# State tokens' products with the data's high and low words side by side, and a reordered end of the layer-one stage, in an attention and two-layer MoE kernel

## The chip, the cores and the metric

The kernel runs on one core of one Trainium2 chip. The metric is device time in microseconds of one execution, the median of several runs. Engines are named as in the profile: PE is TensorE's matmul, PEld its weight load, DVE is VectorE, ACT is ScalarE, POOL is GpSimd, SP is SyncE, which here issues most DMAs (SPq is its queue).

## What is computed

Inputs are `x` (8, 8, 512, 64) and `state` (8, 8, 32, 64): 8 batch entries, 8 heads, 512 ordinary tokens and 32 state tokens each. The reference, cut to its core:

```python
# attention, per batch entry and head
xread = softmax(x @ state.T / 8) @ state       # 512 tokens
sread = softmax(state @ x.T / 8) @ x           # 32 state tokens
x = concat(xread, sread)                       # to (4352, 512): 8 * 544 tokens
# first layer
h = np.maximum(x @ w_in, 0.0)                  # w_in  512 x 2048
x = h * h @ w_out                              # w_out 2048 x 512
# second layer
a = x @ w1                                     # 512 x 1024
b = x @ w2                                     # 512 x 1024
out = ((a * b) @ w3) @ w_out2                  # 1024 x 1024, 1024 x 512
```

Everything is float32 (weights reach the kernel as float64). The kernel keeps float32 precision by splitting a number into a high word and a low word (both float32r, a type of which TensorE takes one column in one pass) and adding three products: high times high, low times high, high times low.

## The kernel before, in words

**Tokens.** The 8 x 512 ordinary tokens are the batches c = 0 to 7, with tiles 512 columns wide. The 8 x 32 = 256 state tokens of all batch entries form a ninth batch, c = B = 8, with tiles 256 columns wide (NT9). The change touches the products of c = B alone.

**Splits and passes.** `split` (L80) makes a ScalarE copy that rounds to the high word (L81) and a VectorE subtraction that gives the low word (L82). `PASSES` (L84) lists the three pairs of words. Split tiles are 128 x 2 x 512, high words in the first half, low words in the second.

**Layer one.** `h_tile(c, f)` (L477) makes one of 16 tiles of hidden units. For c = B (L493 to L502) it splits the 512 x 128 piece of w_in, then does 4 products over k, three matmuls of 256 columns each, into half a PSUM bank of the pair "h". `act_h` (L469) then does Relu out of PSUM, Square, and a split into `ghl`. `y_tile(c, f)` (L513) multiplies with w_out's row f into four banks y0 to y3, three matmuls for each d, and at the last f copies each bank to a tile `yo` (two buffers), from which it is stored to DRAM (`y_scr`). The loop over `order` (L717) keeps y two tiles behind h with the list `pend`; after the loop two y tiles are left in it.

**The product w34 = w3 @ w_out2.** `w3_split(kk)` (L749) splits one of eight rows of the transposed w3 into two tiles, which share two buffers each (tags sw0 and sw1) with the w_in pieces. `w34_rows(kk)` (L763) does 24 matmuls of 512 columns into a bank of the pair "h", splits the result, and after each second row makes sums and differences that go to DRAM (`w34u`). The eight rows are taken in the loop at L1206; while one is multiplied, the next is split. Before that loop, the two y tiles left are done (L1203). Halfway, `make_w` (L829) splits the first half of w1 and w2 with their sums.

**Layer two.** It runs in two passes s = 0, 1, each over half of the 1024 inner units. Ordinary batches are taken in pairs with a Strassen-like scheme: `load_pair` and `make_pair` (L854, L863; 14 splits and 8 differences) make the right sides, `quad` (L941) multiplies into banks qa, qd, qe and qc, `out_pair` (L1071) multiplies with w34. The state tokens go ahead of the pairs: `load9` (L984) reads their y from DRAM, `make9` (L992) splits it into `z` tiles, `ab9(m)` (L1000, m = 0 to 3) makes a and b as two times four products in two banks of y0 to y3 (two m at a time hold banks), and multiplies them: a ScalarE copy of the first bank, a VectorE product with the second, and a split. `out9` (L1030) multiplies the four results with w34. In pass 0, `load9` puts its data into tag s0 of pool `bp`, which is opened (L1216) over the memory that w34's pool leaves.

**What sets the order.** The instructions of each engine run in one fixed order, made when the kernel is built: a scheduler takes them by their place in the text, and lets a later one go ahead where an earlier one isn't ready by its own estimate. `tc.issue_after(ins)` keeps a block's instructions on the engine of `ins` behind `ins`. At run time each engine is strictly in order, and so is SP's queue of DMAs, each of which waits at the head until its buffers are ready.

Of the kernel before, what the change touches and what calls it, by code (L numbers as in the profile page):

```python
# [20 lines left out]
def kernel(  # L21
# [17 lines left out]
    nc = tc.nc  # L39
# [428 lines left out]

    def act_h(c, f, ph, n):  # L469
        r = pa.tile([P, 512], F32, tag="r", bufs=2, name="r")  # L470
        nc.scalar.activation(r[:, :n], ph[:, :n], ACTF.Relu)
        t = pa.tile([P, 2, 512], F32R, tag="ghl", bufs=3, name="ghl")
        nc.scalar.activation(r[:, :n], r[:, :n], ACTF.Square)  # L473
        done.append(split(t[:, HI, :n], t[:, LO, :n], r[:, :n]))
        g_t[c, f] = t

    def h_tile(c, f):  # L477
        ph = bank_h(f"ph{c}_{f}_")
        if c < B:
            fg, m = f // 4, f % 4  # L480
            k = 0
            for g in range(G):
                s, a = SW[c, fg, g], aT_t[c, g]
                for wi, ai in PASSES:
                    mm = nc.tensor.matmul(
                        ph, s[:, wi, m * P:(m + 1) * P], a[:, ai, :],
                        start=(k == 0), stop=(k == 3 * G - 1),
                    )
                    k += 1
            h_mms.append(mm)  # L490
            act_h(c, f, ph, 512)
        else:
            cols = slice((f % 4) * P, (f % 4 + 1) * P)  # L493
            t = pa.tile([P, 2, ND, P], F32R, tag=f"sw{f % 2}", bufs=2, name="w9")
            split(t[:, HI], t[:, LO], win_t[f // 4][:, :, cols])
            for k in range(ND):
                for i, (wi, xi) in enumerate(PASSES):
                    nc.tensor.matmul(
                        ph[:, :NT9], t[:, wi, k, :], x9_t[k // 2][:, xi, k % 2, :],
                        start=(k == 0 and i == 0), stop=(k == ND - 1 and i == 2),  # L500
                    )
            act_h(c, f, ph, NT9)  # L502

    x9_t = []

# [7 lines left out]
    def y_tile(c, f):  # L513
        n = 512 if c < B else NT9
        part, (f0, f1) = [(i, sg) for i, sg in enumerate(segs[c]) if sg[0] <= f < sg[1]][0]
        if f == f0:
            for d in range(ND):
                y_ps[c, d] = bank_y(d, f"y{d}")
        if wo_t[f] is None:
            close_splits()  # L520
        t = g_t.pop((c, f))
        for d in range(ND):
            for k, (wi, gi) in enumerate(PASSES):
                nc.tensor.matmul(  # L524
                    y_ps[c, d][:, :n], wo_t[f][:, wi, d * P:(d + 1) * P], t[:, gi, :n],
                    start=(f == f0 and k == 0), stop=(f == f1 - 1 and k == 2),
                )
            if f == f1 - 1:
                pool, tag = (pa, "yo") if d < 2 or c >= B - 1 else (att, "yo2")
                o = pool.tile([P, 512], F32, tag=tag, bufs=2, name="yo")  # L530
                if d % 2 and c > 1:
                    nc.vector.tensor_copy(o[:, :n], y_ps[c, d][:, :n])
                else:
                    nc.scalar.copy(o[:, :n], y_ps[c, d][:, :n])
                nc.sync.dma_start(y_scr[c][part][:, d, :], o[:, :n])
# [213 lines left out]
    def w3_split(kk):  # L749
        src = stage["w3", kk].rearrange("p h (d k q) -> p k (h d) q", d=2, q=NS)  # L750
        for half in range(2):
            t = pa.tile([P, 2, 4, 4, NS], F32R, tag=f"sw{half}", bufs=2, name="w3T")
            split(t[:, HI], t[:, LO], src[:, 4 * half:4 * half + 4])
            w3T[kk, half] = t.rearrange("p s k d q -> p s (k d q)")

    NH = DM // 2
    NB = N1 // 4
# [242 lines left out]
    def ab9(m):  # L1000
        pss = [bank_y(2 * i + m % 2, "ab") for i in range(2)]
        for i in range(2):
            for d in range(ND):
                w = W[f"A{i + 1}{d // 2 + 1}", d % 2]
                for k, (wi, vi) in enumerate(PASSES):
                    nc.tensor.matmul(  # L1006
                        pss[i][:, :NT9], w[:, wi, m * P:(m + 1) * P], Y[B, d][:, vi, :NT9],
                        start=(d == 0 and k == 0), stop=(d == ND - 1 and k == 2),
                    )
        a = bp.tile([P, 512], F32, tag="s0", bufs=2, name="a")  # L1010
        nc.scalar.copy(a[:, :NT9], pss[0][:, :NT9])
        nc.vector.tensor_tensor(out=a[:, :NT9], in0=pss[1][:, :NT9], in1=a[:, :NT9], op=ALU.mult)
        if m % 2 == 0:
            left["c9"] = z_tile(5 if m == 0 else 1, "c9").rearrange("p h (d n) -> p d h n", d=2)
        t = c_t[B, m] = left["c9"][:, m % 2]
        split(t[:, HI], t[:, LO], a[:, :NT9])

    o_scr = {}
    o_in = {}
# [180 lines left out]

    rows = list(range(N1 // 2, N1)) + list(range(N1 // 2))
    w3_split(rows[0])
    while pend:  # L1203
        y_tile(*pend.pop(0))
    raw = load_w(0)
    for i, kk in enumerate(rows):  # L1206
        if i + 1 < N1:
            w3_split(rows[i + 1])
        if i + 4 < N1:
            load_w3(rows[i + 4])  # L1210
        w34_rows(kk)
        if i == 3:
            for job in make_w(raw):
                job()
# [1 line left out]
    bp = ctx.enter_context(tc.tile_pool(name="bp", bufs=1, reuse_waits="tile"))  # L1216

    turns = [(3, 4), (5, 6), (7, 2), (0, 1)]
    raw9 = load9(bp, "s0")
    raw = load_pair(*turns[0])  # L1220
    make9(raw9)
    while rest:
        rest.pop()()
    for job in make_pair(raw):
        job()
    for s, todo in enumerate((turns, turns[::-1])):
        if s == 1:
            for t in range(NT9 // P):
# [56 lines left out]
```

## Time and profile before

| what | value |
|---|---|
| median of 3 runs | 1220.3 us (1218.64 to 1220.49) |
| the profiled execution's own time | 1219.03 us |
| its span, first to last instruction | 1217.3 us |
| granted TensorE clock, mean | 0.999 of full speed |
| DMA | 150.66 MB moved, 124 GB/s mean |
| stage of the state tokens' layer one | about 612 to 667 us |
| stage of w34 | about 667 to 712 us |
| ab9 and out9, pass 0 | 715 to 733 us |
| ab9 and out9, pass 1 | 963 to 981 us |

The profile is of one execution; times in it count from its first instruction. A row of the timeline gives the start, how long the merged instructions take, the engine, the line, the operation and its tiles; a wait ahead of the row stands in brackets, with the instruction that ended it. "Mean ns" of a matmul includes its way through the pipeline, so that matmuls which follow each other closely overlap in it.

### The profile page before, as it was taken

What the parts mean: (1) busy time and instruction counts of PE and PEld (TensorE: products, weight loads), DVE (VectorE), ACT (ScalarE), POOL (GpSimd) and SP (SyncE); (2) the same over time, 40 slices, a digit from 0 to 9 for tenths busy, and PEclk for the clock granted to TensorE, in tenths of its full rate; (3) what the DMA queues carried; (4) which work ended last, traced back from release to release, by engine and by line L of the source; (5) the groups of instructions that cost most, each with busy time, mean ns of one, the idle gap of its engine ahead of it and who ended that gap; (6) DMA issues with size and microseconds to landing.
All of it is one profiled execution on the core that took longest, in us unless ns stands there. A gap on an engine that the chain in (4) does not pass through costs nothing.

```text
span 1217.3 us, 18891 instructions
## 1 busy us (share of the span) xinstructions
PE 1201.4 (99%) x7174; PEld 999.6 (82%) x7174; DVE 869.4 (71%) x1594; ACT 662.2 (54%) x1220; POOL 109.4 (9%) x163
## 2 busy tenths in 40 slices
PE   7999999999999999999999999999999999999998
PEld 5677777777778777778899888989898989898988
DVE  6968877677586766742435875878696957877877
ACT  6877466555464655654656653546363635453542
POOL 0000001322421121100000000000000000211110
PEclk9999999999999999999999999999999999999999
DMA  9445664835446397630413642223232540716244
GB/s 260 138 140 173 159 184 145 185 113 130 129 127 156 106 184 155 154 53 35 121 53 113 222 156 98 81 93 104 70 104 70 191 138 20 155 30 144 49 74 138
DMA packets 147922, 150.66 MB, mean 124 GB/s; under 512 B 81016, under 2 KB 107128, under 8 KB 147320
## 3 DMA queue, kind: packets, MB, share of 16 engines
q1 hardware_dynamic: 120968, 106.20, 29.6%
q0 software_dynamic: 26576, 43.00, 15.6%
q8 instruction: 56, 0.92, 0.3%
q14 instruction: 34, 0.28, 0.1%
q10 hardware_dynamic: 288, 0.26, 0.1%
HBM read 99.61 MB, written 55.05 MB: 127 GB/s over the span
## 4 chain that ended last, share of the span: by engine, by line
PE 89%; DMA 4%; DVE 3%; ACT 3%; SPq 1%; issue 0%; DVEq 0%; ACTq 0%
PE y L524 29%; PE qa L945 11%; PE qd L945 7%; PE oa L1096 5%; PE od L1096 4%; PE qc L945 4%; PE qe L945 4%; PE ps_sw L454 2%; PE ab L1006 2%; PE oe L1096 2%; PE oc L1096 2%; DMA yraw<-yscr 1%; DMA raw<-in_moe_w_in_dram 1%; PE po L1036 1%; PE ps_r L400 1%; PE ps_s L320 1%
## 5 line engine op out<-in xcount | busy, mean ns | idle before, releaser
L524 PE MATMUL y<-ghl,wo 128*128 128x512 f32 (+1 forms) x1728 | 398.9, 380 | 0.5 <-ACT ghl L81 0.5
L524 PEld LDWEIGHTS y<-ghl,wo 128*128 128x128 f32 x1728 | 310.3, 188 | 74.9 <-issue 13.4
L82 DVE TENSOR_TENSOR ghl<-r,ghl 128x512 fp32r<-128x512 f32 (+1 forms) x144 | 95.1, 660 | 163.2 <-ACT ghl L81 138.7
L953 ACT COPY s<-qa 128x512 f32<-128x512 f32 x96 | 56.5, 589 | 180.1 <-PE qa L945 179.3
L945 PE MATMUL qa<-yq,wq 128*128 128x512 f32 x576 | 143.7, 389 | 0.0
L945 PEld LDWEIGHTS qa<-yq,wq 128*128 128x128 f32 x576 | 107.7, 188 | 22.0
L945 PE MATMUL qd<-yq,wq 128*128 128x512 f32 x384 | 97.4, 389 | 0.0
L82 DVE TENSOR_TENSOR z<-q,z 128x512 fp32r<-128x512 f32 x112 | 74.3, 687 | 23.7 <-ACT z L81 23.6
L473 ACT ACTIVATE r<-r 128x512 f32<-128x512 f32 (+1 forms) x144 | 87.7, 609 | 3.2
L81 ACT CAST ghl<-r 128x512 fp32r<-128x512 f32 (+1 forms) x144 | 86.0, 597 | 3.6
L945 PEld LDWEIGHTS qd<-yq,wq 128*128 128x128 f32 x384 | 72.1, 188 | 15.0
L1136 POOL DMA_DIRECT2D out_dram<-o x24 | 28.6, 1597 | 598.2 <-DVE o L1126 598.0
L81 ACT CAST z<-q 128x512 fp32r<-128x512 f32 x112 | 68.1, 625 | 20.2 <-PE oe L1096 7.4
L957 DVE TENSOR_TENSOR s<-qa,s 128x512 f32<-128x512 f32 x32 | 22.1, 692 | 69.8 <-ACT s L953 69.8
L82 DVE TENSOR_TENSOR yq<-yraw,yq 128x512 fp32r<-128x512 f32 x98 | 64.6, 686 | 4.2 <-ACT yq L81 4.2
L81 ACT CAST yq<-yraw 128x512 fp32r<-128x512 f32 x98 | 59.3, 625 | 12.5 <-DVE yraw L874 7.6
L945 PE MATMUL qe<-yq,wq 128*128 128x512 f32 x192 | 48.7, 389 | 0.0
L945 PE MATMUL qc<-yq,wq 128*128 128x512 f32 x192 | 48.7, 389 | 0.0
L770 PE MATMUL ps_w<-wo,w3T 128*128 128x512 f32 x192 | 44.0, 390 | 0.3 <-ACT u L81 0.3
L899 DVE TENSOR_TENSOR q<-q,q 128x512 f32<-128x512 f32 x64 | 43.1, 684 | 0.0
L770 PEld LDWEIGHTS ps_w<-wo,w3T 128*128 128x128 f32 x192 | 35.9, 188 | 8.1 <-ACT u L81 0.7
L945 PEld LDWEIGHTS qc<-yq,wq 128*128 128x128 f32 x192 | 36.0, 188 | 7.5
(598 smaller groups left out, 2059.5 us busy)
## 6 DMA issues: line engine op xcount, KB each, us to landing
yraw<-yscr SPq DMA_DIRECT2D x56, 256.0 KB, 5.4
yscr<-yo SPq DMA_DIRECT2D x52, 256.0 KB, 3.1
raw<-in_moe_w_out_dram SPq DMA_DIRECT2D x16, 512.0 KB, 4.3
raw<-in_moe_w_dram POOLq DMA_DIRECT2D x64, 128.0 KB, 3.5
raw<-in_moe_w_dram POOLq DMA_DIRECT2D x16, 512.0 KB, 5.0
raw<-in_moe_w_in_dram SPq DMA_DIRECT2D x12, 512.0 KB, 4.2
out_dram<-o SPq DMA_DIRECT2D x24, 256.0 KB, 2.7
out_dram<-o POOLq DMA_DIRECT2D x24, 256.0 KB, 6.6
```

The costliest lines, as they stand in the source:

```text
L81: nc.scalar.copy(hi, src)
L82: return nc.vector.tensor_tensor(out=lo, in0=src, in1=f32(hi), op=ALU.subtract)
L454: mm = nc.tensor.matmul(pss[r][k * NS:(k + 1) * NS, cols], stT[rows, b, k, :], win_t[fg][rows, k, cols], start=True, stop=True, tile_posit ...
L473: nc.scalar.activation(r[:, :n], r[:, :n], ACTF.Square)
L524: nc.tensor.matmul(y_ps[c, d][:, :n], wo_t[f][:, wi, d * P:(d + 1) * P], t[:, gi, :n], start=(f == f0 and k == 0), stop=(f == f1 - 1 and k ...
L770: nc.tensor.matmul(ps, t[:, wi, (j % 4) * P:(j % 4 + 1) * P], wo2_t[j][:, vi, :], start=(j == 0 and k == 0), stop=(j == N1 - 1 and k == 2),)
L899: return nc.vector.tensor_tensor(out=t, in0=a, in1=b, op=ALU.subtract)
L945: nc.tensor.matmul(ps, W[w, kt][:, wi, m * P:(m + 1) * P], Y[v, kt][:, vi, :], start=(first and kt == 0 and k == 0), stop=(last and kt == ...
L953: left["copy"] = nc.scalar.copy(t, ps)
L1006: nc.tensor.matmul(pss[i][:, :NT9], w[:, wi, m * P:(m + 1) * P], Y[B, d][:, vi, :NT9], start=(d == 0 and k == 0), stop=(d == ND - 1 and k ...
L1096: nc.tensor.matmul(ps[tp][:, t % 2 * NH:(t % 2 + 1) * NH], Z[v, idx][:, vi, t * P:(t + 1) * P], rhs[:, wi], start=(first and t % 2 == 0 an ...
L1136: nc.gpsimd.dma_start(dst, src, accum_op=ALU.add)
```

## The change

Products of state tokens use a new function `wide`. It loads the weights' high words once and streams the data's high and low words side by side, 512 columns, into both halves of a bank; then it loads the weights' low words and streams the data's high words, 256 columns, onto the second half. The two halves are added where the bank is read: a ScalarE copy of the first half and a VectorE addition of the second, in `act_h`, in `y_tile`'s last step and in `ab9` (for each of the two banks). In the w34 loop, the first row of w34 and the split of the second row of w3 come ahead of the two y tiles left in `pend`. `load9` of pass 0 uses the buffers of `yo`. The VectorE work of the first pair's `make_pair` is kept behind the last split of w3.

```diff
--- before.py
+++ after.py
@@ -468,7 +468,12 @@
 
     def act_h(c, f, ph, n):
         r = pa.tile([P, 512], F32, tag="r", bufs=2, name="r")
-        nc.scalar.activation(r[:, :n], ph[:, :n], ACTF.Relu)
+        if c == B:
+            nc.scalar.copy(r[:, :n], ph[:, :n])
+            nc.vector.tensor_tensor(out=r[:, :n], in0=ph[:, n:], in1=r[:, :n], op=ALU.add)
+            nc.scalar.activation(r[:, :n], r[:, :n], ACTF.Relu)
+        else:
+            nc.scalar.activation(r[:, :n], ph[:, :n], ACTF.Relu)
         t = pa.tile([P, 2, 512], F32R, tag="ghl", bufs=3, name="ghl")
         nc.scalar.activation(r[:, :n], r[:, :n], ACTF.Square)
         done.append(split(t[:, HI, :n], t[:, LO, :n], r[:, :n]))
@@ -494,12 +499,15 @@
             t = pa.tile([P, 2, ND, P], F32R, tag=f"sw{f % 2}", bufs=2, name="w9")
             split(t[:, HI], t[:, LO], win_t[f // 4][:, :, cols])
             for k in range(ND):
-                for i, (wi, xi) in enumerate(PASSES):
-                    nc.tensor.matmul(
-                        ph[:, :NT9], t[:, wi, k, :], x9_t[k // 2][:, xi, k % 2, :],
-                        start=(k == 0 and i == 0), stop=(k == ND - 1 and i == 2),
-                    )
+                wide(ph, lambda wi: t[:, wi, k, :], x9_t[k // 2][:, :, k % 2, :], k == 0, k == ND - 1)
             act_h(c, f, ph, NT9)
+
+    def wide(ps, w, v, first, last):
+        n = v.shape[2]
+        nc.tensor.matmul(
+            ps.rearrange("p (i n) -> p i n", i=2), w(HI), v, start=first, stop=False, skip_group_check=True,
+        )
+        nc.tensor.matmul(ps[:, n:], w(LO), v[:, HI], start=False, stop=last, skip_group_check=True)
 
     x9_t = []
 
@@ -520,7 +528,10 @@
             close_splits()
         t = g_t.pop((c, f))
         for d in range(ND):
-            for k, (wi, gi) in enumerate(PASSES):
+            cols = slice(d * P, (d + 1) * P)
+            if c == B:
+                wide(y_ps[c, d], lambda wi: wo_t[f][:, wi, cols], t[:, :, :n], f == f0, f == f1 - 1)
+            for k, (wi, gi) in enumerate(PASSES if c < B else ()):
                 nc.tensor.matmul(
                     y_ps[c, d][:, :n], wo_t[f][:, wi, d * P:(d + 1) * P], t[:, gi, :n],
                     start=(f == f0 and k == 0), stop=(f == f1 - 1 and k == 2),
@@ -528,7 +539,10 @@
             if f == f1 - 1:
                 pool, tag = (pa, "yo") if d < 2 or c >= B - 1 else (att, "yo2")
                 o = pool.tile([P, 512], F32, tag=tag, bufs=2, name="yo")
-                if d % 2 and c > 1:
+                if c == B:
+                    nc.scalar.copy(o[:, :n], y_ps[c, d][:, :n])
+                    nc.vector.tensor_tensor(out=o[:, :n], in0=y_ps[c, d][:, n:], in1=o[:, :n], op=ALU.add)
+                elif d % 2 and c > 1:
                     nc.vector.tensor_copy(o[:, :n], y_ps[c, d][:, :n])
                 else:
                     nc.scalar.copy(o[:, :n], y_ps[c, d][:, :n])
@@ -750,8 +764,9 @@
         src = stage["w3", kk].rearrange("p h (d k q) -> p k (h d) q", d=2, q=NS)
         for half in range(2):
             t = pa.tile([P, 2, 4, 4, NS], F32R, tag=f"sw{half}", bufs=2, name="w3T")
-            split(t[:, HI], t[:, LO], src[:, 4 * half:4 * half + 4])
+            last = split(t[:, HI], t[:, LO], src[:, 4 * half:4 * half + 4])
             w3T[kk, half] = t.rearrange("p s k d q -> p s (k d q)")
+        return last
 
     NH = DM // 2
     NB = N1 // 4
@@ -1002,18 +1017,17 @@
         for i in range(2):
             for d in range(ND):
                 w = W[f"A{i + 1}{d // 2 + 1}", d % 2]
-                for k, (wi, vi) in enumerate(PASSES):
-                    nc.tensor.matmul(
-                        pss[i][:, :NT9], w[:, wi, m * P:(m + 1) * P], Y[B, d][:, vi, :NT9],
-                        start=(d == 0 and k == 0), stop=(d == ND - 1 and k == 2),
-                    )
-        a = bp.tile([P, 512], F32, tag="s0", bufs=2, name="a")
-        nc.scalar.copy(a[:, :NT9], pss[0][:, :NT9])
-        nc.vector.tensor_tensor(out=a[:, :NT9], in0=pss[1][:, :NT9], in1=a[:, :NT9], op=ALU.mult)
+                wide(pss[i], lambda wi: w[:, wi, m * P:(m + 1) * P], Y[B, d], d == 0, d == ND - 1)
+        ab = bp.tile([P, 512], F32, tag="s0", bufs=2, name="ab")
+        a, b = ab[:, :NT9], ab[:, NT9:]
+        for v, ps in ((a, pss[0]), (b, pss[1])):
+            nc.scalar.copy(v, ps[:, :NT9])
+            nc.vector.tensor_tensor(out=v, in0=ps[:, NT9:], in1=v, op=ALU.add)
+        nc.vector.tensor_tensor(out=a, in0=b, in1=a, op=ALU.mult)
         if m % 2 == 0:
             left["c9"] = z_tile(5 if m == 0 else 1, "c9").rearrange("p h (d n) -> p d h n", d=2)
         t = c_t[B, m] = left["c9"][:, m % 2]
-        split(t[:, HI], t[:, LO], a[:, :NT9])
+        split(t[:, HI], t[:, LO], a)
 
     o_scr = {}
     o_in = {}
@@ -1200,15 +1214,15 @@
 
     rows = list(range(N1 // 2, N1)) + list(range(N1 // 2))
     w3_split(rows[0])
-    while pend:
-        y_tile(*pend.pop(0))
     raw = load_w(0)
     for i, kk in enumerate(rows):
         if i + 1 < N1:
-            w3_split(rows[i + 1])
+            turned_w3 = w3_split(rows[i + 1])
         if i + 4 < N1:
             load_w3(rows[i + 4])
         w34_rows(kk)
+        while pend:
+            y_tile(*pend.pop(0))
         if i == 3:
             for job in make_w(raw):
                 job()
@@ -1216,13 +1230,14 @@
     bp = ctx.enter_context(tc.tile_pool(name="bp", bufs=1, reuse_waits="tile"))
 
     turns = [(3, 4), (5, 6), (7, 2), (0, 1)]
-    raw9 = load9(bp, "s0")
+    raw9 = load9(pa, "yo")
     raw = load_pair(*turns[0])
     make9(raw9)
     while rest:
         rest.pop()()
-    for job in make_pair(raw):
-        job()
+    with tc.issue_after(turned_w3.ins):
+        for job in make_pair(raw):
+            job()
     for s, todo in enumerate((turns, turns[::-1])):
         if s == 1:
             for t in range(NT9 // P):
```

## Rows read from the trace of the kernel before

**Rows 1.** The page, part 1: busy time (share of the span) and instructions of each engine

```profile
PE 1201.4 (99%) x7174; PEld 999.6 (82%) x7174; DVE 869.4 (71%) x1594; ACT 662.2 (54%) x1220; POOL 109.4 (9%) x163
```

**Rows 2.** The page, part 4: shares of the span of the chain that ended last

```profile
PE 89%; DMA 4%; DVE 3%; ACT 3%; SPq 1%; issue 0%; DVEq 0%; ACTq 0%
```

**Rows 3.** Waits of PE from 600 us on: waiter, releaser, total us, times, longest

```profile
PE ab L1006 <- ACT y9q L81: 1.1, 1, 1.1
PE y L524 <- ACT ghl L81: 0.5, 1, 0.5
PE ps_w L770 <- ACT u L81: 0.3, 1, 0.3
```

**Rows 4.** The chain that ended last, in order of time: start us, us, step

```profile
727.42 5.47 PE po L1036 x24
...
757.37 2.72 PE qa L945 x12
...
771.12 5.76 PE od L1096 x48
...
963.18 8.64 PE ab L1006 x72
```

**Rows 5.** Timeline, 634 to 642 us: one state tile, f = 6

```profile
634.82 1.60 PE L498 MATMUL ph__6307<-x,w 128*128 128x256 f32 x12
...
638.14 0.43 DVE L82 TENSOR_TENSOR ghl<-r,ghl 128x256 fp32r<-128x256 f32 x1
...
642.02 1.60 PE L524 MATMUL y<-ghl,wo 128*128 128x256 f32 x12
```

**Rows 6.** Timeline, 662 to 668 us: the last y tiles and w34's start

```profile
662.18 3.04 PE L524 MATMUL y<-ghl,wo 128*128 128x256 f32 x24
...
665.71 1.99 PE L524 MATMUL y<-ghl,wo 128*128 128x256 f32 x12 [0.50 <-ACT ghl L81]
...
667.54 38.27 PE L770 MATMUL ps_w<-wo,w3T 128*128 128x512 f32 x168
```

**Rows 7.** Timeline, 704 to 707 us: w34's last row

```profile
704.03 0.69 DVE L874 TENSOR_TENSOR yraw<-yraw 128x512 f32<-128x512 f32 x1 [1.79 <-DMA yraw<-yscr]
...
705.57 0.41 DVE L788 TENSOR_TENSOR d<-ps_w,e 128x256 f32<-128x256 f32 x1
...
706.13 5.72 PE L770 MATMUL ps_w<-wo,w3T 128*128 128x512 f32 x24 [0.33 <-ACT u L81]
```

**Rows 8.** Timeline, 711 to 721 us: ab9's start in pass 0

```profile
711.23 1.25 SPq L988 DMA_DIRECT2D y<-yscr  x2
...
711.69 2.88 PE L945 MATMUL qa<-yq,wq 128*128 128x512 f32 x12
...
715.19 1.33 ACT L81 CAST y9q<-y 128x256 fp32r<-128x256 f32 x4 [1.22 <-DMA y<-yscr]
715.63 0.76 DVE L82 TENSOR_TENSOR y9q<-y,y9q 128x256 fp32r<-128x256 f32 x2 [0.83 <-ACT y9q L81]
...
715.65 11.77 PE L1006 MATMUL ab<-y9q,wq 128*128 128x256 f32 x96 [1.08 <-ACT y9q L81]
...
720.33 0.42 DVE L1012 TENSOR_TENSOR a<-ab,a 128x256 f32<-128x256 f32 x1
```

**Rows 9.** Timeline, 963 to 972 us: ab9 in pass 1

```profile
963.02 8.80 PE L1006 MATMUL ab<-y9q,wq 128*128 128x256 f32 x72
...
964.66 0.37 ACT L1011 COPY a<-ab 128x256 f32<-128x256 f32 x1 [3.73 <-PE ab L1006]
...
965.77 1.29 DVE L82 TENSOR_TENSOR wq<-wraw,wq 128x512 fp32r<-128x512 f32 x2
966.97 2.49 DVE L839 TENSOR_TENSOR wraw<-wraw 128x512 f32<-128x512 f32 x4
...
971.79 0.42 DVE L1012 TENSOR_TENSOR a<-ab,a 128x256 f32<-128x256 f32 x1
```

## The prediction

> **What bounds the kernel now.** I read the page first: TensorE is busy 99% of the span, VectorE 71% [rows 1], and the chain that ended last is 89% PE [rows 2]. So time comes off in two ways only: TensorE needs less time for its work, or it waits less. Next come TensorE's waits from 600 us to the end, which hold all that the change touches: three, of 1.1, 0.5 and 0.3 us [rows 3]. The reader is to see how little there is to win from waits. For the work itself I use the chain, because its merged steps give the pitch (start to start), while a matmul's own mean duration covers its pipeline. A step of 48 matmuls of 256 columns takes 5.76 us, 120.0 ns each; ab9's 72 take 8.64 us, again 120.0; twelve of 512 columns take 2.72 us, 226.7 ns [rows 4]. The difference, 106.7 ns for 256 columns, is the 2.4 GHz level, and 13.3 ns are left for each instruction at either width. The timeline then shows where the three waits lie and what fills VectorE there.
>
> **The change, part by part.**
>
> *Side-by-side products.* Each product of a state tile was three matmuls of 256 columns, 360.0 ns; it becomes one of 512 and one of 256, 226.7 + 120.0 = 346.7 ns. The columns stay, one fixed 13.3 ns goes. There are 16 f x 4 products in h_tile, as many in y_tile, and 2 passes x 4 m x 8 in ab9: 192 in all, 192 x 13.3 = **2.56 us less**. The bounds are 0 (below, a rival) and 2.56. For the new matmul's moving data in two pieces of 256 the trace has a likeness: out9's matmuls read their 512 columns in two such pieces and take 5.47 us for 24, 228 ns [rows 4]. So I take all 2.56.
> The Trainium skill ("TensorE: Matmul & The Clock Gate", section "Back-to-back issue gap") has a warm gap of N/2.4 + 2.5 ns, thus 2.5 ns fixed; by it a product would shrink from 327.5 to 325.0 ns, an estimate of 0.5 us over the 192. The pitches just read speak against it.
>
> *What it adds to the state tiles of layer one.* Two halves must be added: a ScalarE copy (0.37 us by the copy in ab9 [rows 9]) and a VectorE add of 256 columns (0.43, as the subtraction of that size [rows 5]) ahead of Relu. In the steady part a tile's products start at 634.82, its low words are done at 638.14 + 0.43 = 638.57, and the second-layer products that need them start at 642.02 [rows 5]: 3.4 us of cover, of which the longer chain takes some 0.9. I cost it at nothing. If ScalarE, which then also splits w1 and w2, runs late for the last tiles, it costs up to 0.5 us once.
>
> *First third-weight row ahead of the last second-layer products.* Now 24 y matmuls start at 662.18, should end at 665.06 (24 x 120.0), and the next start at 665.71: 0.65 lost. Those 12 should end at 667.15, and w34 starts at 667.54: 0.39 lost [rows 6]. (The waits view says 0.5, since it counts the modelled drain as busy.) With a row of 24 x 226.7 = 5.44 us in between, the low words of f = 14 and 15 have that much more time. **1.04 us less.** The row's own needs are covered: its bank of the h pair is free once tile 14 is added up, and both halves of the third weight's first rows are split before. The four evictions of y, now a copy and an add each, free banks that ab9 wants 40 us later.
>
> *VectorE work of the first pair behind the last third-weight split.* At 704.03 VectorE stands 1.79 us at a yraw subtraction that waits for its DMA, so the sums that free a w34 bank end only at 705.57 + 0.41, and the last row's products start at 706.13 [rows 7]. The 168 before it started at 667.54 [rows 6] and should end 38.08 us later, at 705.62: 0.51 lost. Behind the last split the pair's work can no longer stand ahead of that eviction: **0.51 us less**. Late next is the pair itself: its 22 VectorE instructions (14 splits, 8 differences, 0.62 each by four L839 in 2.49 [rows 9]). The last split reuses the buffers of the row two before its own, whose products will end two rows (10.9 us) ahead of the last row's end, worked out below as 708.3; so the pair starts near 699. ScalarE's casts are not held back.
>
> *load9 into yo.* Its two DMAs are issued at 711.23, behind w34's stores on SP's queue and into memory that w34p held; ScalarE has the data at 715.19, and ab9 starts at 715.65 [rows 8]. Twelve qa matmuls fill from 711.69 to 714.41, so 1.24 us are lost. yo is free once y's last stores have landed, and y's products will end seven rows (38.1 us) before w34's, so the data is there when the z tiles (over w34p's memory) come free: **1.24 us less**. The first wide matmul needs low words too (0.38 us each, by y9q's pair in 0.76 [rows 8]); the qa matmuls cover that. What sits behind load9 on SP's queue (third-weight loads for the fifth row on, w34's stores, pair loads) waits for the landing of y's stores; I cost it at nothing, as the first four rows, 21.8 us of products, were loaded before. POOL's queue isn't passed.
>
> *ab9's evictions.* This is where the change costs. Before, a first bank (i = 0) came free by a ScalarE copy alone, the second by VectorE's product. Now each bank needs a copy and a VectorE add, and VectorE is full of work that stands earlier in the kernel. Per m that is one copy and two adds more.
> First pass: the last w34 row, which ended at 706.13 + 5.44 = 711.57, ends 1.7 (128 shorter products) + 1.04 + 0.51 earlier, near 708.3. qa (2.72) and m = 0 and 1 (2 x 8 x 0.347 = 5.55) fill until 716.6; the add for m = 0 must be done by then. Lower bound 0: its data is there some 3 us sooner, and before, the product of m = 0 came at 720.33, 1.6 us after its matmuls (715.65 + 24 x 0.12, and 0.2 of drain) [rows 8]. Upper bound: from 699 us, 22 x 0.62 + 3 w34 evictions x 0.62 + some 22 short ones x 0.38 = 23.9 us of earlier work without a gap end at 722.9, 6.3 us late. I take 0.5, near the lower end, as that row is this very place: VectorE had gaps there, waiting for ScalarE's casts.
> Second pass: ab9 starts at 963.02; m = 0 and 1 end 5.55 later, at 968.57; qa can fill 2.72, to 971.29. VectorE is full there with the splits and sums of w1 and w2 (from 965.77 and 966.97, end to end), and the product of m = 0, whose matmuls ended near 966, came at 971.79 [rows 9]. An add in its place frees the bank at 972.2. Bounds: 0 (the add slips in earlier) and 3.6 (no qa in between). I take 1.0.
> Last m: copy 0.37, add 0.42, product 0.42, cast and subtraction 0.4 each, with the hand-overs 2.4 us until out9 has the low words of m = 3; its nine matmuls on m = 0 to 2 last 2.04. 0.4 in each pass, 0.8.
>
> **Sum**: -2.56 - 1.04 - 0.51 - 1.24 = -5.35; + 0.5 + 1.0 + 0.8 = +2.3; net -3.05 us. The profiled execution took 1219.03 us, so 1216.0; the median of the runs shown is 1.27 above it, so against 1220.3 I forecast 1217.2.
>
> **Rivals.**
> *No new waits.* ab9's adds slip in and only the gains stand: 1220.3 - 5.35 = 1215.0. For it: in the first pass VectorE has gaps, and qa matmuls are there to fill. Against it: the full stretch of the second pass.
> *The waits eat most of it.* The second pass finds no qa between (3.6) and the first loses 1: -5.35 + 4.6 + 0.8 = 0.05, thus about 1220, and within 0.2% anywhere from 1218 on. For it: the product of m = 0 came 5.6 us after its data.
> *Two pieces cost twice.* If the 13.3 ns belong to each contiguous piece of moving data, the wide matmul takes 240 ns and 2.56 goes: 1219.8. By the formula of the Trainium skill's page "TensorE: Matmul & The Clock Gate", section "Back-to-back issue gap", 2.1 of the 2.56 would go, an estimate of 1219.3, in the same case. Against it: out9's 228 ns.
> *VectorE holds ab9's banks in the first pass* (the other side). Held back to 699 us, the pair's 22 instructions run packed ahead of the adds, and ab9 stands for the upper bound of 6.3 us; with 3.0 in the second pass and 0.8 at out9 that is +10.1 - 5.35 = +4.75, 1225. It decides once new waits pass 5.35 us, and past 0.2% once they pass 7.8. For it: all this work stands earlier in the kernel than ab9. Against it: the gaps by ScalarE's casts [rows 8].
>
> **How the numbers follow.** About 0.2% (2.4 us) is what a measurement of this kernel can tell from no change. Forecast 0.40 and no new waits 0.16 are faster; waits eat most of it 0.24 and two pieces 0.08 are the same; VectorE in the first pass is slower, 0.12. So faster 0.56, same 0.32, slower 0.12. The range goes from 1214.6, just under all gains, to 1221.0, past the cases of no change; nearly all of the slower case and a little of the others stay outside.
>
> **What would show it.** Right: 64 matmuls of 512 and 64 of 256 at each of L498's, L524's (state) and L1006's places with 0.347 us a product; no wait at the y products near 665 nor at the last w34 row; y9q's cast following the last w34 row without a DMA wait; a wait of ab's third group on VectorE in the second pass of about 1 us, less than that in the first. Wrong: a pitch of 240 ns for the wide matmul; PE waits on VectorE in ab9 that sum to over 5 us; a new wait of the w34 rows on their loads, which would say that load9 blocked SP's queue; or the stall before ab9 still there, if the z tiles or VectorE and not the load set it.

## The result and the profile after

The changed kernel takes 1226.37 us (median of six runs, 1224.57 to 1227.97) against 1219.91 for the kernel before (six runs beside them): ratio 1.0056, 95% interval 1.0043 to 1.0069. It is 6.5 us slower, where 3 us less was forecast. The profiled execution took 1227.29 us, its span is 1225.5.

From the page: busy time, and the shares of the chain that ended last.

```profile
PE 1202.7 (98%) x6982; PEld 991.1 (81%) x6982; DVE 882.8 (72%) x1628; ACT 672.6 (55%) x1246; POOL 109.4 (9%) x163
...
PE 90%; DVE 6%; DMA 2%; ACT 1%; issue 1%; SPq 0%; DVEq 0%; ACTq 0%
```

TensorE has 192 matmuls less than before (7174 in [rows 1]) and yet 1.3 us more of busy time: some of its time ran at a lower clock, as will be seen. In the chain, VectorE's share has gone from 3% [rows 2] to 6%, and ScalarE's and the DMAs' have shrunk. The waits of TensorE from 600 us on, in the same view as [rows 3]:

```profile
PE ab L507 <- DVE ab L1025: 5.7, 3, 4.5
PE ab L507 <- DVE y9q L82: 1.7, 1, 1.7
```

All three waits of before are gone: for ScalarE's y9q cast, for the last state tiles, for w34's last row. In their place stand three waits for the addition that frees a bank of ab9, 5.7 us in all, and one of 1.7 us for y9q's low words.

To see where the 8.2 us of span arose (1225.5 against 1217.3), the chain of each kernel is cut at steps which both have. Of the kernel after (start us, us, step):

```profile
612.96 2.72 PE y L535 x12
...
732.39 5.75 PE po L1050 x24
753.10 2.72 PE qa L960 x12
937.40 2.72 PE qa L960 x12
...
1004.87 2.72 PE qa L960 x12
...
1189.17 2.72 PE qa L960 x12
```

The same view of the kernel before (its po step at 727.42 is in [rows 4]):

```profile
612.13 2.72 PE y L524 x12
...
747.85 2.72 PE qa L945 x12
932.15 2.72 PE qa L945 x12
997.89 2.72 PE qa L945 x12
1182.19 2.72 PE qa L945 x12
```

The first step is the last y tile of an ordinary batch; up to there nothing was changed, and 0.83 us lie in the same instructions. From it to the qa matmuls ahead of ab9 (711.69 in [rows 8], 709.16 after, shown below) the change **gains 3.36 us**: 99.56 becomes 96.20. From those qa matmuls to out9's first step in pass 0 it **loses 7.50 us**: 727.42 - 711.69 = 15.73 becomes 732.39 - 709.16 = 23.23. The pairs of both passes take 184.30 us in either kernel. From the last pair of pass 0 to the first of pass 1, the stretch of the second ab9, it **loses 1.73 us**: 65.74 becomes 67.47. Of the rest, 0.3 us lie between out9 and the first pair, and 1.2 us behind the last pair: there the same instructions run up to the last four stores of the output, but these land 3.1 us after their issue, where before it was 1.8.

**Where the gain comes from.** Timeline, the state tiles' products:

```profile
651.63 0.39 PE L507 MATMUL ph__6457<-x,w 128*128 128x512 f32 x1
...
651.98 0.39 PE L507 MATMUL ph__6457<-x,w 128*128 128x512 f32 x1
```

From one wide matmul to the next it is 0.35 us, as 0.347 was worked out: two pieces of 256 columns cost no more than one of 512.

**Where the loss lies.** Timeline of the kernel after, from the qa matmuls to the first product that waits for a bank:

```profile
709.16 2.88 PE L960 MATMUL qa<-yq,wq 128*128 128x512 f32 x12
709.52 0.57 ACT L81 CAST w<-ps_w 128x512 fp32r<-128x512 f32 x1
709.99 1.33 ACT L81 CAST y9q<-y 128x256 fp32r<-128x256 f32 x4
710.16 1.29 DVE L889 TENSOR_TENSOR yraw<-yraw 128x512 f32<-128x512 f32 x2
711.36 0.69 DVE L82 TENSOR_TENSOR yq<-yraw,yq 128x512 fp32r<-128x512 f32 x1
...
711.97 0.68 DVE L82 TENSOR_TENSOR w<-ps_w,w 128x512 fp32r<-128x512 f32 x1
712.57 0.41 DVE L802 TENSOR_TENSOR d<-ps_w,e 128x256 f32<-128x256 f32 x1
712.90 0.41 DVE L803 TENSOR_TENSOR d<-ps_w,e 128x256 f32<-128x256 f32 x1
...
713.70 0.50 PE L507 MATMUL ab<-y9q,wq 128*128 128x512 f32 x1 [1.66 <-DVE y9q L82]
...
715.42 0.37 ACT L1024 COPY ab<-ab 128x256 f32<-128x256 f32 x1 [2.00 <-PE ab L510]
...
719.34 0.28 PE L510 MATMUL ab<-y9q,wq 128*128 128x256 f32 x1
...
719.92 0.69 DVE L889 TENSOR_TENSOR yraw<-yraw 128x512 f32<-128x512 f32 x1
720.53 1.89 DVE L82 TENSOR_TENSOR yq<-yraw,yq 128x512 fp32r<-128x512 f32 x3
...
723.54 0.42 DVE L1025 TENSOR_TENSOR ab<-ab 128x256 f32<-128x256 f32 x1
...
724.10 0.77 PE L507 MATMUL ab<-y9q,wq 128*128 128x512 f32 x1 [4.48 <-DVE ab L1025]
```

Two stalls. First, y9q's casts wait for no DMA any more, but they stand behind the cast of w34's last row, and their subtractions behind pair work and that row's three VectorE steps; the qa matmuls end at 711.9 and ab9 starts at 713.70. Second, the copy of m = 0's first bank is done at 715.8, but VectorE comes to the addition only at 723.54, 7.7 us later: the subtractions and splits of the first pair (yraw, yq) stand ahead of it, and among them the sums of w34's last row. What that did to the clock shows in the table of windows (us, busy us and instructions of PE, PEld, DVE, ACT, POOL, then the granted clock, DMA share, GB/s):

```profile
709.16:713.70 4.54, 2.88 (x14) 2.07 (x12) 4.54 (x10) 3.19 (x8) 0.00 (x0) 1.00 0.01 2
713.70:719.50 5.80, 5.80 (x32) 4.89 (x32) 5.80 (x15) 3.70 (x9) 0.00 (x0) 1.00 0.22 90
719.50:724.10 4.60, 0.12 (x1) 0.03 (x1) 4.60 (x9) 2.75 (x5) 0.00 (x0) 0.85 0.28 114
724.10:729.40 5.30, 5.30 (x17) 4.53 (x18) 3.40 (x9) 1.18 (x3) 0.00 (x0) 0.50 0.78 214
729.40:732.39 2.99, 2.99 (x18) 2.64 (x18) 1.61 (x4) 1.62 (x4) 0.00 (x0) 0.98 0.86 314
```

VectorE is busy in every microsecond from 709.16 to 724.10. Behind the 4.6 us in which TensorE had nothing to do, its granted clock is 0.50 for 5.3 us, the 1.2 GHz level: the last 16 products take 8.29 us to out9's first step instead of 16 x 0.347 = 5.55, thus 2.7 more. The loss in pass 0 is then 1.8 + 4.6 + 2.7 = 9.1 us, against 1.2 us of wait that [rows 8] had there and 0.4 by 32 shorter products: 7.5.

The Trainium skill ("TensorE: Matmul & The Clock Gate", section "What's actually happening") says that the throttled clock is the default and that activity releases it, with levels of 1.2 and 2.4 GHz; the window behind the stall agrees, at 0.50.

### The profile page after: what moved, and what is told of

It is laid out like the page before. It is cut to its first block, busy times and chain, and to the rows that moved or that the text cites. A ratio compares the mean times of both kernels' runs of the same rounds, so it can differ in the third digit from the quotient of the medians.

```text
span 1225.5 us, 18541 instructions
## 1 busy us (share of the span) xinstructions
PE 1202.7 (98%) x6982; PEld 991.1 (81%) x6982; DVE 882.8 (72%) x1628; ACT 672.6 (55%) x1246; POOL 109.4 (9%) x163
## 4 chain that ended last, share of the span: by engine, by line
PE 90%; DVE 6%; DMA 2%; ACT 1%; issue 1%; SPq 0%; DVEq 0%; ACTq 0%
PE y L535 28%; PE qa L960 10%; PE qd L960 7%; PE oa L1110 5%; PE qc L960 4%; PE qe L960 4%; PE od L1110 3%; PE ps_sw L454 2%; PE ps_w L785 2%; PE oe L1110 2%; PE oc L1110 1%; PE y L507 1%; PE po L1050 1%; DMA raw<-in_moe_w_in_dram 1%; DVE wq L82 1%
## 5 line engine op out<-in xcount | busy, mean ns | idle before, releaser
L535 PE MATMUL y<-ghl,wo 128*128 128x512 f32 x1536 | 372.4, 391 | 0.0
L535 PEld LDWEIGHTS y<-ghl,wo 128*128 128x128 f32 x1536 | 286.1, 188 | 73.4 <-issue 13.4
L785 PE MATMUL ps_w<-wo,w3T 128*128 128x512 f32 x192 | 43.9, 390 | 0.0
L960 PEld LDWEIGHTS qe<-yq,wq 128*128 128x128 f32 x192 | 36.0, 188 | 7.5
```

Of the source, the lines that this page charges most:

```text
L535: nc.tensor.matmul(y_ps[c, d][:, :n], wo_t[f][:, wi, d * P:(d + 1) * P], t[:, gi, :n], start=(f == f0 and k == 0), stop=(f == f1 - 1 and k ...
L785: nc.tensor.matmul(ps, t[:, wi, (j % 4) * P:(j % 4 + 1) * P], wo2_t[j][:, vi, :], start=(j == 0 and k == 0), stop=(j == N1 - 1 and k == 2),)
L960: nc.tensor.matmul(ps, W[w, kt][:, wi, m * P:(m + 1) * P], Y[v, kt][:, vi, :], start=(first and kt == 0 and k == 0), stop=(last and kt == ...
```

## The experiments

The theory: layer one gains what was forecast; ab9 loses because the held-back pair work runs as one block on VectorE, ahead of the additions that free ab9's banks, and the idle time costs clock on top. Rivals: the two-step evictions alone are at fault, without the hold; or the reordering alone (first row ahead, load into yo, hold) is, without the wide products. All were timed in five rounds. "Stretch" is the time from the last ordinary y tile to the last pair's qa step of the profiled execution, 570.06 us before and 576.21 after; it leaves out the start, where equal instructions differed by up to 2.4 us between executions, and the end. Differences of medians are against the kernel before in the same session.

**No hold** (no_gate): the kernel after, with the pair's work where the scheduler puts it.

```diff
-    with tc.issue_after(turned_w3.ins):
-        for job in make_pair(raw):
-            job()
+    for job in make_pair(raw):
+        job()
```

> The changed kernel with the first pair's VectorE work no longer kept behind the last w3 split. Theory (ab9's banks wait for VectorE adds that stand behind earlier work, and the 4.6 us of idle TensorE then let its clock fall to half): the pair's work spreads out again ahead of 699 us, so the 4.6 us wait of ab in pass 0 shrinks to 1 to 2 us, the half clock goes with it, and the last w34 row waits its 0.5 us again; about 1221 us beside 1219.9 before. Rival (the wide matmuls or the added evictions cost by themselves, whatever the order): 1226 us, the same PE wait.

Measured: 1220.6 us, ratio 1.0012 [1.0002, 1.0021]: of 6.5 us of loss 1.6 are left (stretch +0.6). The waits of TensorE from 600 us on:

```profile
PE ab L507 <- DVE y9q L82: 1.9, 1, 1.9
PE ab L507 <- DVE ab L1025: 1.2, 2, 0.7
```

Both waits for the additions lie in pass 1; in pass 0 no bank is waited for. The first addition starts at 719.69, 3.9 us earlier than in the kernel after; the first products also ran at a lower clock (the window stands in the last section), which made that bank due some 1.6 us later, an estimate from their starts. So the two-step evictions are late only where VectorE is full, and in pass 0 it was the hold that filled it.

**ScalarE frees the banks** (act_frees): the kernel after, but each bank is copied whole by ScalarE and its halves added from there.

```diff
-        ab = bp.tile([P, 512], F32, tag="s0", bufs=2, name="ab")
-        a, b = ab[:, :NT9], ab[:, NT9:]
-        for v, ps in ((a, pss[0]), (b, pss[1])):
-            nc.scalar.copy(v, ps[:, :NT9])
-            nc.vector.tensor_tensor(out=v, in0=ps[:, NT9:], in1=v, op=ALU.add)
+        ab = [bp.tile([P, 512], F32, tag=tag, bufs=2, name="ab") for tag in ("s0", "qb")]
+        a, b = (v[:, :NT9] for v in ab)
+        for v, ps in zip(ab, pss):
+            nc.scalar.copy(v, ps)
+            nc.vector.tensor_tensor(out=v[:, :NT9], in0=v[:, NT9:], in1=v[:, :NT9], op=ALU.add)
```

> The changed kernel with ab9's banks copied whole by ScalarE and both halves added from SBUF, so that VectorE frees no bank. It has as many VectorE instructions and longer ScalarE copies. Theory: the waits on VectorE in ab9 go (4.6 us in pass 0, 1.3 us in pass 1) and the half clock with them (2.7 us), about 1217.8 us. Rival (VectorE's added load itself): no gain, 1225 to 1227 us.

Measured: 1219.56 us, ratio 1.0005 [0.9997, 1.0014], with the hold still in, so the theory and not the rival, if 1.8 us short of it. Waits:

```profile
PE ab L507 <- DVE y9q L82: 2.1, 1, 2.1
PE po L1050 <- ACT c L81: 1.2, 1, 1.2
```

No wait for a bank is left in either pass. What remains of VectorE's block shows where the forecast had put 0.4 us, at out9: 1.2 us in pass 0. VectorE's place in the path of freeing the banks was thus what the hold made dear.

**The pair's work behind ab9** (late_pair): the kernel after, with only the first two of the seven pair jobs (which fill the qa matmuls) ahead of ab9 in the text, and the other five behind ab9 in pass 0.

```diff
+    pair_jobs = make_pair(raw)
     with tc.issue_after(turned_w3.ins):
-        for job in make_pair(raw):
+        for job in pair_jobs[:2]:
             job()
...
+        if s == 0:
+            for job in pair_jobs[2:]:
+                job()
```

> The changed kernel, but of the first pair's work only the first two jobs (B11 and T1) stand ahead of ab9 in the text; the other five follow ab9, so that the scheduler takes ab9's VectorE adds first. Nothing is left out. Theory (the adds wait because 14 of the pair's instructions stand ahead of them): the 4.6 us wait and the 2.7 us of half clock in pass 0 go, pass 1 keeps its 1.7 us, about 1219 us beside 1219.2 before and 1226 for the changed kernel. Rival (VectorE has too much to do, so the wait only moves): quad's products wait instead, 1222 us or more.

Measured: 1219.91 us, ratio 1.0002 [0.9993, 1.0010] (stretch -1.1). The timeline in pass 0, and the windows over the same time:

```profile
716.03 0.42 DVE L1025 TENSOR_TENSOR ab<-ab 128x256 f32<-128x256 f32 x1
```

```profile
713.50:719.00 5.50, 5.50 (x33) 4.75 (x33) 5.45 (x15) 3.18 (x8) 0.00 (x0) 1.00 0.32 126
719.00:725.00 6.00, 6.00 (x36) 5.21 (x35) 5.31 (x13) 3.76 (x9) 0.00 (x0) 1.00 0.19 73
```

The first addition comes at 716.03 instead of 723.54, TensorE has no gap, the clock stays at 1.00. The instructions are those of the kernel after, and the two jobs ahead are still held; the other five come behind ab9, so only the order differs. This shows the mechanism directly, and the other traces agree with it: of the pair's 22 VectorE instructions, 21 stand ahead of VectorE's first read of an ab9 bank in every kernel that holds them all back, 15 or 16 in every kernel without the hold, and 11 here.

**Before's ab9 in the kernel after** (old_ab9), and **the reordering without any wide product** (order_only):

```diff
-                wide(pss[i], lambda wi: w[:, wi, m * P:(m + 1) * P], Y[B, d], d == 0, d == ND - 1)
+                for k, (wi, vi) in enumerate(PASSES):
...
+        nc.vector.tensor_tensor(out=a[:, :NT9], in0=pss[1][:, :NT9], in1=a[:, :NT9], op=ALU.mult)
```

```diff
-    while pend:
-        y_tile(*pend.pop(0))
...
+            turned_w3 = w3_split(rows[i + 1])
...
+        while pend:
+            y_tile(*pend.pop(0))
...
+    raw9 = load9(pa, "yo")
...
+    with tc.issue_after(turned_w3.ins):
```

> The changed kernel with ab9 as before (three matmuls of 256 columns, a first bank freed by ScalarE); layer one wide and all reordering kept. Theory: waits and half clock of ab9 go (8.6 us), 0.85 us of shorter products go back, and of the 1.8 us wait for low words of y9 over 1 us goes: about 1217 us. Rival (the reordering, with the pair's work held back, is what hurts): over 1222 us, with VectorE still ending the waits of ab.

> The kernel before with the reordering alone (first w34 row ahead of the last two y tiles, load9 into yo, the first pair's VectorE work behind the last w3 split), all products as before. Theory: the three waits of TensorE go, 1.04 + 0.51 + 1.24 us less, about 1217 us. Rival (the held-back VectorE work costs in ab9 even with the old evictions): 1220 us or more.

Measured: old_ab9 1219.84 us, ratio 1.0007 [0.9999, 1.0016], between its theory and its rival: VectorE still ends two waits of ab, 1.8 us for the product of a and b and 1.3 us for y9q's low words, and ScalarE's cast of y9q a third of 1.3 us. order_only took **1223.57 us, 1.0029 [1.0019, 1.0040]**, 4.5 us slower than before; not the theory but its rival came. Its waits:

```profile
PE ab L1007 <- DVE a L1013: 2.1, 1, 2.1
PE ab L1007 <- DVE y9q L82: 1.2, 1, 1.2
PE ab L1007 <- ACT y9q L81: 0.9, 1, 0.9
PE ps_w L771 <- ACT u L81: 0.2, 1, 0.2
```

L1013 is before's VectorE product of a and b: it too reads a bank and so frees it, and the hold makes it late even with no addition added. The sum is 4.4 us of waits against 1.9 before [rows 3], and the stretch is 2.6 us longer; the rest of the 4.5 lies ahead of it or in chance. So the hold makes a bank wait with before's ab9 too, and not only with the wide one; the wide one has its first addition due earlier, and waits 4.5 us where this one waits 2.1.

**The hold alone** (gate_only): the kernel before with nothing but `issue_after` around the pair's jobs, as in the diff above.

> The kernel before with one edit: the first pair's VectorE work behind the last w3 split. Theory (this is what costs, also with the old ab9): 2 to 4 us more than before, 1221.5 to 1223 us, with waits of ab on VectorE in pass 0. Rival (in order_only the moved row or the moved load cost it): 1219 us or less, the 0.5 us of the last w34 row gained.

Measured: 1221.53 us, ratio 1.0010 [1.0001, 1.0019]; the one large wait is again for that product:

```profile
PE ab L1007 <- DVE a L1013: 2.0, 1, 2.0
```

It did what it was priced for: no wait at w34's last row is left. The wait for y9q's cast has gone as well, without any move of the load: its DMAs are issued at 707.86 instead of 711.23 [rows 8]. Both gains together, 1.6 us by [rows 3] and [rows 7], went into the product's wait. By its trace it comes out even (stretch +0.2), by medians 1.8 us behind; that difference one profile doesn't place.

**Wide products of layer one alone** (wide_l1_only): the kernel before with `wide` in `h_tile` and `y_tile` and the additions in `act_h` and `y_tile`; no other part.

```diff
+        if c == B:
+            nc.scalar.copy(r[:, :n], ph[:, :n])
+            nc.vector.tensor_tensor(out=r[:, :n], in0=ph[:, n:], in1=r[:, :n], op=ALU.add)
+            nc.scalar.activation(r[:, :n], r[:, :n], ACTF.Relu)
...
+                wide(ph, lambda wi: t[:, wi, k, :], x9_t[k // 2][:, :, k % 2, :], k == 0, k == ND - 1)
...
+                wide(y_ps[c, d], lambda wi: wo_t[f][:, wi, cols], t[:, :, :n], f == f0, f == f1 - 1)
```

> The kernel before with side-by-side products in layer one alone (h_tile and y_tile), no reordering, ab9 as before. Theory: 128 products save 13.3 ns each and their longer evictions are covered: 1.7 us less, about 1217.3 us beside 1219.0. Rival (the added ScalarE and VectorE work delays the last tiles): 1219 us or more, with longer waits of the y products near 665 us.

Measured: **1216.5 us, ratio 0.9975 [0.9965, 0.9985]** (stretch -3.4): the lowest median of all versions (the two that follow lie within the noise of it) and faster than both kernels. The one wait left, and the timeline where layer one ends:

```profile
PE ab L1021 <- ACT y9q L81: 0.3, 1, 0.3
```

```profile
661.58 0.28 PE L510 MATMUL y<-ghl,wo 128*128 128x256 f32 x1
661.70 0.39 PE L785 MATMUL ps_w<-wo,w3T 128*128 128x512 f32 x1
...
662.21 0.50 PE L507 MATMUL y<-ghl,wo 128*128 128x512 f32 x1
```

A matmul of w34 (L785) stands between the y products, though the text has all of w34 behind them: given other durations, the scheduler filled the gap by itself. So the moved row was not needed for that gain.

**Layer one with the first row ahead** (l1_row), and **with load9 into yo too** (l1_row_yo); no hold, before's ab9:

```diff
-    while pend:
-        y_tile(*pend.pop(0))
     for i, kk in enumerate(rows):
...
+        while pend:
+            y_tile(*pend.pop(0))
...
-    raw9 = load9(bp, "s0")
+    raw9 = load9(pa, "yo")
```

(The last two lines are in l1_row_yo only.)

> Layer one wide, first w34 row ahead of the last two y tiles; ab9, load9 and the order of the first pair's VectorE work as before. Theory: 1.7 us of products and 1.04 us of waits less, nothing new: about 1216.3 us. Rival (moving the row delays the first pair or w34 itself): 1218 us or more.

> As l1_row, with load9 into yo. As predicted at first, the early load takes 1.24 us off, 1215.1 us. Theory now: the z tiles come free only with the last w34 row, and y9's casts and subtractions then stand behind that row's eviction and the pair's work on ScalarE and VectorE, so the early load gains nothing: 1216 us, with a wait of ab on y9 still there.

Measured: 1217.52 us, 0.9985 [0.9976, 0.9994], and 1217.4 us, 0.9984 [0.9975, 0.9993]. Neither part adds to the gain of wide_l1_only, and where load9 puts its data makes no difference that can be measured: the wait ahead of ab9 is 0.9 us in l1_row and 0.6 us in l1_row_yo.

**The wide ab9 alone** (wide_ab9_only): the kernel before with `wide` and the four-step eviction of the change in `ab9`.

> The kernel before with side-by-side products in ab9 alone. Theory (each bank now waits for a VectorE add behind earlier work, in both passes): +1.7 us in pass 1 as in the changed kernel and 1 to 3 us in pass 0, 0.85 us less for the products, about 1221 to 1223 us. Rival (the wait in pass 0 comes from the held-back pair work alone): no wait in pass 0, 1220 us.

Measured: 1222.35 us, ratio 1.0022 [1.0013, 1.0031]. Its waits:

```profile
PE ab L506 <- DVE ab L1017: 1.2, 2, 0.7
PE ab L506 <- DVE y9q L82: 1.0, 1, 1.0
PE y L531 <- ACT ghl L81: 0.3, 1, 0.3
```

Again the banks are waited for in pass 1 alone (1.2 us). The stretch is only 0.8 us longer, the median 3.1. Of the other 2.3 us, 1.4 stand at the end of its trace: the last stores of the output land 3.3 us after their issue, against 1.8 before. This belongs to the wide ab9 and not to one execution: in all seven kernels that have it these stores take 2.5 to 3.3 us, in all seven with before's ab9 1.7 to 1.9. In the seven with it a 16 KB load of instructions (DMA queue 8) starts 6.2 to 7.7 us ahead of the end, in the others the last one starts 12.4 to 14.2 us ahead; that this load holds up the stores is not shown. The 0.9 us that are left stay open.

**ScalarE's freeing without the hold** (act_nogate: act_frees and no_gate together) and **in before's order** (l1_act: all products wide, banks freed by ScalarE, none of the reordering). Their edits are those above.

> Side-by-side products everywhere, ab9's banks copied whole by ScalarE, first w34 row ahead, load9 into yo, the pair's VectorE work not held back. Theory: no wait on VectorE for banks, no held-back work: the gains of layer one and of the row (about 2.8 us) and some of ab9's 0.85 stand, 1216.5 us. Rival (VectorE's load in ab9 still costs): 1218.5 us or more.

> Side-by-side products everywhere, ab9's banks copied whole by ScalarE, and the order of the kernel before (no row moved, load9 and pair as before). Theory: layer one's 2.8 us as in wide_l1_only, and up to 0.85 us of ab9's products, less the longer wait for y9's low words (about 0.5 us): 1216.2 us. Rival (ab9's longer chain costs more than its products save): 1217.5 us or more.

Measured: 1218.93 us, 0.9992 [0.9982, 1.0002], and 1218.39 us, 0.9983 [0.9974, 0.9992]. Both lie where their rivals had them, though no bank is waited for. Even with free banks a wide ab9 adds nothing to layer one's gain: the 64 products there are worth 0.85 us, but the wait for y9q is 1.5 and 0.9 us in these two, against 0.3 in wide_l1_only, and the last stores land 0.7 and 0.8 us later than there.

**Hold and wide ab9 together.** From l1_row_yo the hold alone leads to old_ab9, the wide ab9 alone to no_gate, both to the kernel after. By medians against before these stand at -1.9, +0.8, +1.6 and +6.5: the hold costs 2.7, the wide ab9 3.5, and both 8.4, more than the sum by 2.2. Each single figure is good to about 1 us, by the intervals, so an excess of 2.2 over four of them is not clear of noise, and by the stretches (-3.6, +1.2, +0.6 and +6.2) it is 0.7. So it isn't shown that the two make each other worse: each costs some 3 to 5 us from l1_row_yo. What is in the kernel after alone is the kind of loss, the bank wait of 4.6 us in pass 0 with its 5.3 us of half clock; old_ab9 and no_gate lose in several shorter waits.

## Why the prediction was wrong

The forecast (1217.2, range to 1221.0) missed; what happened is the rival *VectorE holds ab9's banks in the first pass*, given 0.12 and 1225 us. By its steps:

- **Side-by-side products: right.** 0.347 us forecast, 0.35 measured. Layer one alone gave 2.8 us by medians, where 128 products and the y waits were priced at 1.70 + 1.04 = 2.74. The Trainium skill's formula ("TensorE: Matmul & The Clock Gate", section "Back-to-back issue gap") differs: by it a product would take 325.0 ns, an estimate, and the pitch of 0.35 us speaks against it here. The section gives that formula for an isolated matmul, and says that in a stream the weight loads count too.
- **Added evictions of layer one at nothing: right.** No y product waits for them.
- **First row ahead, last row without a wait: right in size.** With the 128 products -1.70 - 1.04 - 0.51 = -3.25 was forecast for this stretch; -3.36 came. But the row's move was credited with a gain that wide_l1_only had without it, and so was the hold: no_gate and wide_l1_only have no wait at w34's last row either.
- **load9 into yo, -1.24: failed.** The step looked at the DMA, which was indeed last, and not at what is late next. y9q's casts and subtractions go into memory that w34 leaves, and stand behind the last row's eviction and the pair's work; TensorE still waited 1.7 us. That "the qa matmuls cover that" held for the 0.38 us of a subtraction, not for its place in VectorE's order.
- **ab9's evictions in the first pass, +0.5: the step that failed.** The upper bound was worked out nearly right: VectorE done with earlier work at 722.9, 6.3 us late; the first addition began at 723.54, 4.6 us late. That the two ends agree so well is in part luck: the bound let the block begin at 699 with 23.9 us of work; it began at 703.67 and took 19.9. The sign named for this case came as well, 5.7 us of waits of ab on VectorE. I took the lower end because a product in [rows 8] had come in time, between pair work with gaps. But before, that work began on VectorE at 683.72, behind a wait for ScalarE's cast, and lay scattered among w34's rows, nine of its 22 instructions ahead of the last split of w3; held back, it began at 703.67 and ran into ab9 without a gap (14.94 us busy of 14.94 from 709.16 on). The first row is of the kernel before, the second of the kernel after:

```profile
683.72 0.69 DVE L82 TENSOR_TENSOR yq<-yraw,yq 128x512 fp32r<-128x512 f32 x1 [1.43 <-ACT yq L81]
703.67 0.69 DVE L82 TENSOR_TENSOR yq<-yraw,yq 128x512 fp32r<-128x512 f32 x1
```

The row I leaned on belonged to the order that the change removes. late_pair and no_gate take that wait away by order alone.
- **The half clock: not in the sum.** The upper bound had 6.3 us of wait and no price for TensorE's clock behind it; 2.7 us more came. Without it the kernel would still be some 4 us slower.
- **Second pass, +1.0: right as a wait** (0.74 + 0.51 = 1.25 us). The stretch lost 1.73 though its 32 shorter products should have given 0.43. From the pitch of the matmuls ahead of them the two gaps come to 0.97 and 0.68 us, more than the waits view says, since it counts the drain as busy; 0.5 us are then left open.
- **Last m, 0.8: not seen** as a wait of out9 in the kernel after; in act_frees it was 1.2 us in one pass.
- **SP's queue at nothing: right.** No w34 row waited for a load.
- **The end of the kernel: not in the sum.** The last stores took 1.3 us longer to land, as in every kernel with the wide ab9; no step of the prediction looked there.

The sign followed from one choice between two bounds 6.3 us apart, on a change whose whole gain was 5.35. But with that wait taken away (late_pair) the kernel is only even with before, and not 3 us faster: among what is left are 1.3 us of wait for y9q's low words and 1.0 us at the last stores.

## What to carry to other kernels

Fewer and wider matmuls over the same columns pay their fixed time back, but each PSUM bank that must then be read in two steps needs an engine that is free at the right moment: ask where that read stands in the engine's order before asking how long it takes. Holding work back behind an instruction doesn't remove it, it packs it, and whatever stands behind the block in that engine's order becomes late; move the work behind the urgent reads instead, or give those reads to the engine with slack. And a row that shows a step in time, in gaps of an engine, is no evidence once the change removes what made the gaps; price a new stall of TensorE with its clock, not as idle time alone.

## What the runs showed of the hardware that I had not expected

- A stall costs more than its length: 4.6 us without matmuls, then 5.3 us at 0.50, 2.7 us lost again. Shorter stalls went either way: the kernel after kept 1.00 behind its 1.7 us wait, late_pair behind its 1.3 us and act_frees behind its 2.1 us, while no_gate, after a wait of 1.9 us, shows this window:

```profile
713.50:719.00 5.50, 4.46 (x17) 3.82 (x17) 4.52 (x12) 1.91 (x5) 0.00 (x0) 0.69 0.00 0
```

- Profiled executions reached the last ordinary y tile, which no edit had touched, between 611.95 us (wide_l1_only) and 614.37 us (order_only). The granted clock of the first 40 us goes with it: from 30 to 40 us it was 1.00 in the three executions that came first and 0.74 or 0.75 in the three that came last. Of a single profile, only stretches cut at common steps can be compared to better than that.
